# Normalising P one round later in a fused attention and soft-MoE kernel

## The chip, the cores and the metric

The kernel runs on one core of one Trainium2 chip. The time is that of one execution on the device, in microseconds (us); several executions are timed and their median is given. The kernel before takes 286.43 us (three runs, 285.88 to 286.63).

## The reference

Attention in a sliding window of 128 positions with a linear bias per head (ALiBi), for 8 batches, 8 heads, 576 positions, head size 64. Its output, 4608 tokens of 512 numbers, goes through a soft mixture of 8 experts with 4 slots each. Cut to what matters:

```python
scores = scale * q @ k.T + bias                    # masked to 0 <= i-j < 128
attn = exp(scores - max(scores))
attn = attn / (sum(attn) + 1e-9)
x = attn @ v                                       # 4608 x 512
logits = x @ phi                                   # 4608 x 32
d = softmax(logits over tokens); slot_input = d.T @ x
slot_out = relu(slot_input @ w1[e]) @ w2[e]        # for each expert
out = softmax(logits over slots) @ slot_out
```

The change touches the third line only, the division by the sum, and only when it is done.

## The kernel before, in words

The attention is a pipeline over 72 **groups**, nine for each batch: for each of the four full tiles of 128 queries two groups (two of the four blocks of 64 queries and heads at a time), and one for the tail of 64 queries. A group's scores lie in four units of 128 partitions by 128 numbers. The program is a loop of 72 **rounds**; in round i each engine works on other groups, and the order in which each engine gets its instructions is the order of the lines of the program. Every engine runs its own queue in order and waits only for the semaphores of what it reads or overwrites.

Round i, engine by engine:

- VectorE, in `softmax_front`: `merge` (L286) joins the two halves of the window of the scores of group i; `rowmax` (L300) takes the row maximum; `inverse` (L313) inverts the row sums of group i−1; `bias` (L304) makes the bias of the exponentials of group i; `normalise` (L317) multiplies P of group i−1 by the inverted sums. Behind it, when a tile of x is complete, `x_store` (L424) copies it out of its PSUM bank, and in some rounds steps of the mixture follow (L469 a maximum of logits, L496, L536, L537, L522 the accumulation of slot inputs). `filler` puts small leftover steps (L547, L548) between these.
- TensorE: `flip` (L374) transposes P of group i−3, `values` (L410) multiplies P of group i−4 by V, `scores` (L261, L270) computes the scores of group i+1; then transposes of x (L438) and logits (L456) where they are due.
- ScalarE: `split` (L380) copies the transposed P of group i−3 out of PSUM, `x_keep` (L447) and others follow, then `expo` (L359) takes the four exponentials of group i and their sums.
- GpSimd: `total` (L309) adds the epsilon to the sums of group i−1; two affine selects (L386, L388) cut the copied P of group i−3 into the part for the previous block of V and the part for its own.

Three things tie the engines together. There is one PSUM bank for x, so `values` of the next tile waits for `x_store`. There are two buffers for scores, so `scores` of group i+2 waits for `expo` of group i. And `values` waits for both selects, the first half of it for L386 and the second for L388. P itself has three buffers. A constant, `SKIP = 7`, marks the round in which TensorE's flips fall back by one round, so that from round 8 on P of group i−1 isn't flipped before round i+2.

The attention ends at about 212 us of the profiled execution; behind it the last tokens, the experts and the combination follow.

Of the kernel before, what the change touches and what calls it, by code (L numbers as in the profile page):

```python
# [10 lines left out]
F32 = mybir.dt.float32  # L11
# [13 lines left out]
P = 128  # L25
# [20 lines left out]
SKIP = 7  # L46
# [18 lines left out]
def bc(ap, dim, n):  # L65
    ap = ap.unsqueeze(dim)
    shape = list(ap.shape)
    shape[dim] = n
    return ap.to_broadcast(shape)
# [3 lines left out]
def tile_attn_softmoe(  # L73
# [16 lines left out]
    work = ctx.enter_context(tc.tile_pool(name="work", bufs=2))  # L90
# [53 lines left out]
    st = {}  # L144
    last = B - 1

    def order(b):
        return (1, 2, 3, 4, 0) if b == last else range(NT)
# [13 lines left out]
    groups = [(b, t, g) for b in range(B) for t in order(b) for g in range(2 if t < 4 else 1)]  # L162
    number = {key: i for i, key in enumerate(groups)}
    n = len(groups)
# [111 lines left out]
    ALL, LO, HI = slice(0, 4), slice(0, 2), slice(2, 4)  # L276
    EVEN, ODD = slice(0, 4, 2), slice(1, 4, 2)

    def merge(key, us=ALL):
        x = ranges(key, us).rearrange("p a (x y) -> p a x y", y=KB)  # L280
        m = x.shape[1]
        if key[1] < 4:
            to, of, keep = x[:, :, 0:6:5], x[:, :, 2:4], bc(mask.bitcast(I32), 1, m)
        else:
            to, of, keep = x[:, :, 0:8:4], x[:, :, 2:8:4], bc(bc(mask[:, 0].bitcast(I32), 1, 2), 1, m)
        nc.vector.copy_predicated(to, keep, of)  # L286

    def ranges(key, us):
        if number[key] == 0:
            return st[key]["parts"][us.start // 2].unsqueeze(1)  # L290
        return st[key]["s4"]
# [4 lines left out]
    def rowmax(key, us):  # L296
        if "nb" not in st[key]:
            st[key]["nb"] = work.tile([P, 4], F32, tag="nb", name="nb")
        st[key]["mx"] = ranges(key, us)[:, :, 4 * P - 2:4 * P]
        nc.vector.tensor_reduce(st[key]["mx"], merged(key, us), axis=AX.X, op=ALU.max, negate=True)  # L300

    def bias(key, us):
        nb = st[key]["nb"][:, us].rearrange("p (a u) -> p a u", u=2)
        nc.vector.tensor_scalar_mul(nb, st[key]["mx"], SCALE)  # L304

    def total(key, us, eng=None):
        if "rs" not in st[key]:
            st[key]["rs"] = work.tile([P, 4], F32, tag="rs", name="rs")
        (eng or nc.vector).tensor_scalar(  # L309
            st[key]["rs"][:, us], st[key]["sm"][:, us], EPS, 1.0, op0=ALU.add, op1=ALU.mult)  # L310

    def inverse(key, us):
        nc.vector.reciprocal(st[key]["rs"][:, us], st[key]["rs"][:, us])  # L313

    def normalise(key, us):
        p4, rs = st[key]["p4"][:, us], st[key]["rs"][:, us]
        nc.vector.tensor_tensor(p4, p4, bc(rs, 2, P), op=ALU.mult)  # L317

    def normalise_first(key, us):
        p4 = st[key]["p4"]  # L320
        for u in range(4)[us]:
            nc.scalar.mul(p4[:, u], p4[:, u], st[key]["rs"][:, u:u + 1])  # L322
# [3 lines left out]
    def filler():  # L326
        if fillers:
            fillers.pop(0)()

    def softmax_front(new, old):  # L330
        first, eager = number[old] == 0, 0 < number[old] < EAGER
        merge(new)
        filler()
        if not eager:
            total(old, ALL, nc.gpsimd)
        if first:
            inverse(old, ALL)
            normalise_first(old, LO)
        rowmax(new, ALL)
        filler()  # L340
        if not first and not eager:
            inverse(old, ALL)
        filler()
        bias(new, ALL)
        if eager:
            total(old, ALL)
            inverse(old, ALL)
        filler()
        normalise(old, HI if first else ALL)

    def expo(key, us=ALL):
        s = st[key]
# [421 lines left out]
    with tc.manual_schedule(engines=ORDERED):  # L774
        scores(0)
        loads(0)
        for i in range(n):
            new = groups[i]
            run("pre", i)
            if i:  # L780
                softmax_front(new, groups[i - 1])
            else:
                for us in (LO, HI):
                    merge(new, us)
                    rowmax(new, us)
                    bias(new, us)
                    expo(new, us)
            near = int(i < SKIP)
            if i + near >= FLAG and i != SKIP:
                flip(groups[i + near - FLAG])  # L790
                split(groups[i + near - FLAG])
            run("act", i)
            if i + near >= LAG and i != SKIP:
                values(groups[i + near - LAG])
                after_values(i, groups[i + near - LAG])
            if i + 1 < n:
                scores(i + 1)
            if i + 1 < n - 1:
                loads(i + 1)
            if i:  # L800
                expo(new)
            run("pe", i)
            load_weights_at(i)
            run("dve", i)
# [23 lines left out]
        split(gc)  # L828
        token_exp(end)
        total(gd, LO)  # L830
        inverse(gd, LO)
        normalise(gd, LO)
# [296 lines left out]
```

## Time and profile before

| what | value |
|---|---|
| median of three runs | 286.43 us |
| profiled execution, its own time | 286.09 us |
| its span in the profile | 284.3 us |
| TensorE busy | 257.5 us, 91% |
| VectorE busy | 218.6 us, 77% |
| ScalarE busy | 190.5 us, 67% |
| GpSimd busy | 111.7 us, 39% |
| chain of waits, by engine | TensorE 44%, VectorE 38%, ScalarE 9% |

In the profile PE is TensorE, PEld its loading of weights, DVE VectorE, ACT ScalarE, POOL GpSimd. "L317" is line 317 of the kernel before; where a row reads "A <- B: 6.6, 11, 1.0", A waited for B 6.6 us in total, 11 times, at most 1.0 us. In a row of the timeline stand the start, the duration, engine, line and operation, and in brackets how long the engine had been idle before it and who ended that. A share of the whole span says little here, since the last 70 us are other work; the rounds are read in windows of their own.

### The profile page before, as it was taken

Reading aid. Unit: us, or ns where it says so; the run is one execution under the profiler, and the core shown is the slowest. Engines: PE = TensorE matmul, PEld = TensorE weight load, DVE = VectorE, ACT = ScalarE, POOL = GpSimd, SP = SyncE. Lnnn points to the kernel's source line nnn. Section 1 sums busy time; section 2 is a strip of 40 time slices with the busy share of each in tenths; the row PEclk is TensorE's granted clock in tenths of the full one; section 3 lists DMA queues with packets and bytes.
Section 4 is the critical chain, followed back from the end, with each engine's and each line's share of the span. In section 5 each row is a group of like instructions: output and inputs, shape, how many; then the busy total and the mean of one; then the engine's idle time right before and its main releaser. Section 6 shows DMA issues by size and latency. Waiting matters only on the chain.

```text
span 284.3 us, 11675 instructions
## 1 busy us (share of the span) xinstructions
PE 257.5 (91%) x4575; PEld 180.7 (64%) x4575; DVE 218.6 (77%) x546; ACT 190.5 (67%) x780; POOL 111.7 (39%) x221
## 2 busy tenths in 40 slices
PE   7789898989899999998989998998989899999990
PEld 3567676767577677676667766766666443587750
DVE  1789998997998898899999899897973352656352
ACT  2868868887798887897897888887774411044460
POOL 3035734481574385265527526556452011000000
PEclk9999999999999999999999999999999999999996
DMA  5735368889786998889698778876565588999997
GB/s 167 238 110 153 115 173 250 255 247 295 252 277 184 303 303 262 257 265 285 221 298 283 255 236 280 268 212 218 166 213 199 172 257 296 417 416 373 376 357 295
DMA packets 36767, 72.49 MB, mean 255 GB/s; under 512 B 4413, under 2 KB 15337, under 8 KB 36713
## 3 DMA queue, kind: packets, MB, share of 16 engines
q1 hardware_dynamic: 35992, 71.25, 75.7%
q8 instruction: 36, 0.59, 0.8%
q10 hardware_dynamic: 720, 0.51, 0.6%
q14 instruction: 19, 0.15, 0.2%
HBM read 62.30 MB, written 9.44 MB: 252 GB/s over the span
## 4 chain that ended last, share of the span: by engine, by line
PE 44%; DVE 38%; ACT 9%; issue 3%; DMA 3%; POOL 1%; DVEq 0%; ACTq 0%; SPq 0%; POOLq 0%
DVE area L317 12%; DVE s L300 9%; PE xp L410 8%; ACT area L359 6%; PE op L967 5%; PE s L270 5%; DVE area L424 5%; PE hp L930 5%; DVE s L286 4%; PE po L992 4%; PE s L261 2%; PE lp L456 2%; PE pq L374 2%; DVE acc L522 2%; DMA area<-v_n 2%
## 5 line engine op out<-in xcount | busy, mean ns | idle before, releaser
L359 ACT ACTIVATE area<-s,nb 128x128 f32<-128x128 f32 x286 | 101.9, 379 | 21.6 <-DVE nb L304 20.2
L410 PE MATMUL xp<-area 128*64 128x128 f32 (+1 forms) x1104 | 71.7, 270 | 9.5 <-DVE area L424 6.6
L410 PEld LDWEIGHTS xp<-area 128*64 128x64 f32 x1104 | 54.5, 137 | 16.4 <-POOL area L388 5.0
L359 ACT ACTIVATION_READ_ACCUMULATOR area<-s,nb 128x1 f32 x286 | 62.2, 218 | 0.0
L317 DVE TENSOR_TENSOR area<-area,rs 128x512 f32<-128x512 f32 (+1 forms) x73 | 59.9, 821 | 1.7 <-ACT area L447 0.4
L270 PE MATMUL s<-kq 64*64 64x192 f32 (+2 forms) x1144 | 57.0, 316 | 0.0
L386 POOL TENSOR_SCALAR_AFFINE_SELECT area<-area 128x512 f32<-128x512 f32 (+1 forms) x57 | 42.7, 748 | 26.9 <-ACT area L380 26.3
L380 ACT COPY area<-pq 128x512 f32<-128x512 f32 (+1 forms) x72 | 42.5, 592 | 16.0 <-PE pq L374 14.3
L300 DVE TENSOR_REDUCE s<-s 128x4 f32<-128x512 f32 (+1 forms) x72 | 50.0, 694 | 2.2
L388 POOL TENSOR_SCALAR_AFFINE_SELECT area<-area 128x512 f32<-128x512 f32 (+1 forms) x57 | 46.5, 817 | 3.9
L270 PEld LDWEIGHTS s<-kq 64*64 64x64 f32 x1144 | 41.2, 139 | 3.4
L309 POOL TENSOR_SCALAR rs<-sm 128x4 f32<-128x4 f32 x70 | 13.5, 193 | 71.2 <-ACT area L359 69.8
L286 DVE COPY_PREDICATED s<-cst,s 128x256 f32<-128x256 int32 (+1 forms) x72 | 30.2, 419 | 4.8 <-PE s L270 4.4
L374 PE MATMUL pq<-unit_r,area 64*128 64x64 f32 x552 | 31.4, 234 | 1.9 <-ACT area L322 1.2
L374 PEld LDWEIGHTS pq<-unit_r,area 64*128 64x128 f32 x552 | 23.0, 140 | 11.6 <-issue 5.0
L261 PE MATMUL s<-ramp,pair_of 64*64 64x384 bf16 x286 | 27.0, 358 | 2.5 <-ACT area L359 2.0
L424 DVE COPY area<-xp 128x512 f32<-128x512 f32 (+1 forms) x38 | 24.1, 633 | 3.6 <-PE xp L410 3.4
L447 ACT COPY area<-pq 128x512 f32<-128x512 f32 x34 | 20.2, 594 | 0.3 <-PE pq L432 0.3
L261 PEld LDWEIGHTS <-pair_of 64*64 64x64 bf16 x288 | 9.5, 106 | 15.7 <-issue 12.0
L438 PEld LDWEIGHTS pq<-unit_r,area 64*128 64x128 f32 x264 | 10.7, 138 | 13.2 <-issue 11.7
L994 ACT COPY ob<-po 128x512 f32<-128x512 f32 x19 | 10.4, 592 | 11.4 <-PE po L992 11.4
L994 DVE COPY ob<-po 128x512 f32<-128x512 f32 x17 | 11.2, 686 | 6.6 <-PE po L992 4.4
(164 smaller groups left out, 276.6 us busy)
## 6 DMA issues: line engine op xcount, KB each, us to landing
w<-w SPq DMA_DIRECT2D x53, 512.0 KB, 5.4
out<-ob SPq DMA_DIRECT2D x36, 256.0 KB, 3.6
kq<-q_t SPq DMA_DIRECT2D x69, 128.0 KB, 3.3
kq<-k_t SPq DMA_DIRECT2D x32, 256.0 KB, 3.4
area<-v_n SPq DMA_DIRECT2D x31, 256.0 KB, 4.5
area<-w SPq DMA_DIRECT2D x8, 512.0 KB, 4.9
area<-v_n SPq DMA_DIRECT2D x12, 128.0 KB, 5.2
kq<-w SPq DMA_DIRECT2D x3, 512.0 KB, 5.6
```

Source lines behind the costliest of these rows:

```text
L261: nc.tensor.matmul(dst[strip], lhsT=pair_of[rows, int(t == 0), strip], rhs=src, start=True, stop=False)
L270: nc.tensor.matmul(parts[par][KB * jj:KB * jj + KB, second * u + KB * skip:second * u + WIN], lhsT=qt[rows, jj if t < 4 else j, KB * h:KB ...
L286: nc.vector.copy_predicated(to, keep, of)
L300: nc.vector.tensor_reduce(st[key]["mx"], merged(key, us), axis=AX.X, op=ALU.max, negate=True)
L317: nc.vector.tensor_tensor(p4, p4, bc(rs, 2, P), op=ALU.mult)
L359: nc.scalar.activation(s["p4"][:, u], src, AF.Exp, bias=s["nb"][:, u:u + 1], scale=SCALE, accum_out=s["sm"][:, u:u + 1],)
L374: nc.tensor.transpose(s["pt"][:, 2 * (u % 2) + u // 2, r], s["p4"][rows, u], ident[rows, rows])
L380: nc.scalar.copy(pa[:, us].rearrange("p u (r w) -> p u r w", r=2), s["pt"][:, us])
L386: nc.gpsimd.affine_select(prev, own, [[-step, m], [0, 4], [-1, KB]], ALU.is_gt, 0.0, base=-i0, channel_multiplier=1)
L388: nc.gpsimd.affine_select(own, own, [[step, m], [0, 4], [1, KB]], ALU.is_ge, 0.0, base=i0, channel_multiplier=-1)
L410: nc.tensor.matmul(xp[D * par:D * par + D, j, 0:w], lhsT=v_slot[b, t - 1 + ph][:, D * h:D * h + D], rhs=src[:, :, par, i] if t < 4 else sr ...
L424: nc.vector.tensor_copy(dst, src[:, :, 0:w])
```

## The change

The normalisation of P of group i−1 leaves its place behind the bias of round i. It is done in round i+1, behind the merge and in front of the row maximum of group i+1. This holds for rounds after round 8: round 8 has no normalisation at all, and round 71, the last, has two, the moved one behind its merge and the one of group 70 in the old place. The inverted sums live one round longer and get a third buffer. Lines of the changed kernel are four higher from L350 on (L424 is L428 there).

```diff
     def total(key, us, eng=None):
         if "rs" not in st[key]:
-            st[key]["rs"] = work.tile([P, 4], F32, tag="rs", name="rs")
+            st[key]["rs"] = work.tile([P, 4], F32, tag="rs", name="rs", bufs=3)
...
     def softmax_front(new, old):
         first, eager = number[old] == 0, 0 < number[old] < EAGER
+        late = number[new] > SKIP
         merge(new)
+        if number[new] > SKIP + 1:
+            normalise(groups[number[old] - 1], ALL)
         filler()
...
         filler()
-        normalise(old, HI if first else ALL)
+        if not late or number[new] == n - 1:
+            normalise(old, HI if first else ALL)
```

VectorE's queue in rounds 8 and 9, before. `s_0` and `s_1` are the two score buffers, `nb` the bias, `rs` the sums, `xp` the bank of x; both operands of L317 that read `area` are P.

```order
L286 COPY_PREDICATED s_0_83<-cst,s_0_83 128x4x64
L300 TENSOR_REDUCE s_0_83<-s_0_83 128x2x2
L313 RECIPROCAL rs<-rs 128x4
L304 TENSOR_SCALAR nb<-s_0_83 128x4
L317 TENSOR_TENSOR area<-area,rs 128x512
L286 COPY_PREDICATED s_1_84<-cst,s_1_84 128x2x2x64
L300 TENSOR_REDUCE s_1_84<-s_1_84 128x2x2
L313 RECIPROCAL rs<-rs 128x4
L304 TENSOR_SCALAR nb<-s_1_84 128x4
L317 TENSOR_TENSOR area<-area,rs 128x512
L424 COPY area<-xp 128x512
```

The same two rounds in the changed kernel:

```order
L286 COPY_PREDICATED s_0_83<-cst,s_0_83 128x4x64
L300 TENSOR_REDUCE s_0_83<-s_0_83 128x2x2
L313 RECIPROCAL rs<-rs 128x4
L304 TENSOR_SCALAR nb<-s_0_83 128x4
L286 COPY_PREDICATED s_1_84<-cst,s_1_84 128x2x2x64
L317 TENSOR_TENSOR area<-area,rs 128x512
L300 TENSOR_REDUCE s_1_84<-s_1_84 128x2x2
L313 RECIPROCAL rs<-rs 128x4
L304 TENSOR_SCALAR nb<-s_1_84 128x4
L428 COPY area<-xp 128x512
```

Round 8 has lost its L317; in round 9 L317 stands between merge and row maximum, and the store of x follows the bias.

VectorE's queue in round 71, the last of the loop, with the semaphores that each instruction waits for, before:

```order
L286 COPY_PREDICATED s_1_84<-cst,s_1_84 128x2x2x64 [waits PE_49]
L300 TENSOR_REDUCE s_1_84<-s_1_84 128x2x2 [waits DVE_49]
L313 RECIPROCAL rs<-rs 128x4 [waits Pool_49]
L304 TENSOR_SCALAR nb<-s_1_84 128x4 [waits DVE_49]
L317 TENSOR_TENSOR area<-area,rs 128x512 [waits DVE_49,Activation_49]
L469 TENSOR_REDUCE nm<-lg 64x1 [waits Activation_49]
```

And in the changed kernel:

```order
L286 COPY_PREDICATED s_1_84<-cst,s_1_84 128x2x2x64 [waits PE_49,Activation_49]
L317 TENSOR_TENSOR area<-area,rs 128x512 [waits DVE_49]
L300 TENSOR_REDUCE s_1_84<-s_1_84 128x2x2 [waits DVE_49]
L313 RECIPROCAL rs<-rs 128x4 [waits Pool_49]
L304 TENSOR_SCALAR nb<-s_1_84 128x4 [waits DVE_49]
L317 TENSOR_TENSOR area<-area,rs 128x512 [waits DVE_49,Activation_49]
L473 TENSOR_REDUCE nm<-lg 64x1 [waits Activation_49]
```

One L317 has come in front of the row maximum, and the old one has stayed. The merge now names ScalarE too: the exponentials of two rounds before, which read the same score buffer. The other four engines' queues are as they were.

## The prediction

> **What bounds the kernel now.** I read the windows first, then who waits for whom, then the costliest groups, then single rounds in order of time. The windows below cut out the part in which the change acts (columns: length, then busy time of PE, weight load, VectorE, ScalarE, GpSimd; the granted clock is 1.00 throughout).
>
> ```profile
> 28.00:44.00 16.00, 14.41 (x307) 10.65 (x305) 14.48 (x34) 12.54 (x55) 7.42 (x14) 1.00 0.53 157
> 44.00:70.00 26.00, 24.42 (x484) 17.97 (x484) 23.56 (x59) 21.20 (x95) 13.50 (x25) 1.00 0.84 264
> 70.00:95.00 25.00, 23.53 (x465) 17.09 (x465) 22.58 (x59) 20.57 (x90) 13.21 (x26) 1.00 0.78 248
> 95.00:120.00 25.00, 23.86 (x474) 17.32 (x470) 22.88 (x58) 20.80 (x92) 13.81 (x25) 1.00 0.84 271
> 120.00:149.00 29.00, 27.13 (x538) 19.61 (x530) 27.34 (x68) 25.09 (x110) 14.49 (x28) 1.00 0.84 271
> 149.00:175.00 26.00, 24.41 (x486) 18.15 (x486) 24.30 (x60) 21.62 (x95) 14.00 (x26) 1.00 0.84 268
> 175.00:200.00 25.00, 23.90 (x465) 17.34 (x460) 21.25 (x52) 19.11 (x83) 14.90 (x28) 1.00 0.72 223
> ```
>
> TensorE and VectorE are both over 90% busy in most of it, so the end is set by the two in turn. TensorE's idle time is the window less its busy time: 1.59, 1.58, 1.47, 1.14, 1.87, 1.59 and 1.10 us, 10.3 us together. No reordering of VectorE can win more than that. The waits say who owns it.
>
> ```profile
> PE xp L410 <- DVE area L424: 6.6, 11, 1.0
> PEld xp L410 <- POOL area L388: 5.0, 8, 1.1
> ACT area L359 <- DVE nb L304: 20.2, 31, 1.1
> DVE area L424 <- PE xp L410: 3.4, 5, 0.8
> DVE nm L469 <- ACT lg L464: 4.3, 4, 1.5
> L317 DVE TENSOR_TENSOR area<-area,rs 128x512 f32<-128x512 f32 x70 | 58.7, 838 | 1.4 <-ACT area L447 0.4
> ```
>
> The first row is the target: eleven times, 6.6 us in all, the P V product (L410) waits for the store of x (L424) to empty its bank. Before that store VectorE normalises P (L317), 838 ns on average. The second and third rows are what can be hurt: the masks on GpSimd and the exponentials, both downstream of the bias (L304).
>
> **The change part by part.** Nothing is added or removed in work: 63 normalisations (those of P of groups 7 to 69) move from behind the bias to behind the next merge, and round 8 has none. No DMA is moved, and the other engines keep their order. P is flipped two rounds after its exponentials, so the normalised P is still one round early for TensorE.
>
> *Term 1, contention.* The same instruction takes very different times. Three normalisations, and GpSimd's selects beside them:
>
> ```profile
> 132.88 0.69 DVE L317 TENSOR_TENSOR area<-area,rs 128x512 f32<-128x512 f32 x1
> ...
> 28.60 1.15 DVE L317 TENSOR_TENSOR area<-area,rs 128x512 f32<-128x512 f32 x1
> ...
> 33.97 1.12 DVE L317 TENSOR_TENSOR area<-area,rs 128x512 f32<-128x512 f32 x1
> 28.55 0.66 POOL L386 TENSOR_SCALAR_AFFINE_SELECT area<-area 128x512 f32<-128x512 f32 x1 [0.27 <-ACT area L380]
> 29.28 0.99 POOL L388 TENSOR_SCALAR_AFFINE_SELECT area<-area 128x512 f32<-128x512 f32 x1
> ...
> 33.90 0.66 POOL L388 TENSOR_SCALAR_AFFINE_SELECT area<-area 128x512 f32<-128x512 f32 x1
> ```
>
> Alone it takes 0.69 us. At 28.60 and 33.97 it stood behind a select that had begun just before it, and took 0.43 to 0.46 us more; in the first case the next select then waited in turn, 0.99 instead of 0.66. That is no accident: bias, four exponentials, copy, select add up to about a round, so selects fall where the next bias has just ended. Behind the merge, 1.0 us earlier in VectorE's round (0.33 behind the merge's start instead of 1.34, by the rows of term 2), the normalisation mostly misses them. The mean excess is 838 − 690 = 148 ns a round on VectorE, 63 × 0.148 = 9.3 us of its work; bounds 0 (contention follows it) and 9.3.
>
> The Trainium skill, "SBUF — State Buffer", section "Who interferes with whom", has it that a VectorE instruction with two SBUF inputs and a GpSimd instruction that reads SBUF exclude each other for the whole of the one that was first. The rows at 33.90 and 33.97 agree: 33.90 + 0.66 = 34.56, and the late one ended 0.53 behind that. By that rule a meeting in the new place costs as much as one in the old.
>
> *Term 2, a gap that is filled.* The row maximum reads what the merge wrote. A filler that doesn't read it, already there in one round of eight, shows what an instruction costs in between:
>
> ```profile
> 123.83 0.42 DVE L286 COPY_PREDICATED s<-cst,s 128x256 f32<-128x256 int32 x1
> 124.29 0.70 DVE L300 TENSOR_REDUCE s<-s 128x4 f32<-128x512 f32 x1
> 124.89 0.17 DVE L313 RECIPROCAL rs<-rs 128x4 f32<-128x4 f32 x1
> 125.02 0.16 DVE L304 TENSOR_SCALAR nb<-s 128x4 f32<-128x4 f32 x1
> 125.17 0.76 DVE L317 TENSOR_TENSOR area<-area,rs 128x512 f32<-128x512 f32 x1
> 125.85 0.42 DVE L286 COPY_PREDICATED s<-cst,s 128x256 f32<-128x256 int32 x1
> 126.18 0.28 DVE L547 TENSOR_REDUCE cs<-ln 128x4 f32<-128x132 f32 x1
> 126.38 0.68 DVE L300 TENSOR_REDUCE s<-s 128x4 f32<-128x512 f32 x1
> ```
>
> Merge to maximum is 0.46 us bare, but 0.33 to the independent filler. So a normalisation of 0.60 from start to start (0.69 less the overlap of 0.09 that most neighbours show) costs about 0.33 + 0.60 − 0.46 = 0.47 in the new place, 0.60 in the old: 0.13 a round. Bounds 0 and 0.13.
>
> [...]
>
> *The price.* Each bias, and so each set of exponentials, comes 0.47 us later behind its merge. Where VectorE is the late one this changes nothing, because the work has only gone round the loop: the bias then follows the previous store directly. Where the merge itself waited for scores, or where the store waited for TensorE (3.4 us, five times) or the maximum of the logits for ScalarE (4.3 us, four times), the normalisation was cover for that wait; now it stands behind it, and 0.47 is paid on the path bias, exponentials, copy, selects, P V.
>
> *One stretch followed through.* Rounds 8 to 11, row by row:
>
> ```profile
> 28.41 0.13 DVE L304 TENSOR_SCALAR nb<-s 128x4 f32<-128x4 f32 x1
> 28.42 0.51 PE L270 MATMUL s<-kq 64*64 64x64 f32 x16
> 29.67 0.42 DVE L286 COPY_PREDICATED s<-cst,s 128x256 f32<-128x256 int32 x1
> 32.04 0.68 DVE L424 COPY area<-xp 128x512 f32<-128x512 f32 x1
> 32.87 1.09 PE L410 MATMUL xp<-area 128*64 128x128 f32 x16 [0.87 <-DVE area L424]
> 37.43 0.68 DVE L424 COPY area<-xp 128x512 f32<-128x512 f32 x1
> 38.26 1.15 PE L410 MATMUL xp<-area 128*64 128x64 f32 x32 [0.37 <-DVE area L424]
> ```
>
> Round 8 loses its normalisation, so the merge of 29.67 starts once the scores end (28.93) at about 29.0. Its normalisation, at 29.3, still meets the select of 29.28 and ends near 30.5; maximum, reciprocal and bias end at 31.4, and the store starts there instead of at 32.04: P V at 32.2 instead of 32.87. Two rounds on the next store can start at 36.4 instead of 37.43; by then P V waits only for its own queue, and 38.26 becomes 37.25. Gain 1.0 us of the 1.59 that TensorE had idle.
>
> I followed 120 to 175 us the same way. These waits are there for the taking:
>
> ```profile
> 129.51 1.09 PE L410 MATMUL xp<-area 128*64 128x128 f32 x16 [0.97 <-DVE area L424]
> 149.17 1.21 PE L410 MATMUL xp<-area 128*64 128x128 f32 x16 [0.61 <-DVE area L424]
> 154.68 1.09 PE L410 MATMUL xp<-area 128*64 128x128 f32 x16 [0.37 <-DVE area L424]
> 174.60 1.22 PE L410 MATMUL xp<-area 128*64 128x128 f32 x16 [0.57 <-DVE area L424]
> 136.39 1.15 DVE L317 TENSOR_TENSOR area<-area,rs 128x512 f32<-128x512 f32 x1
> ```
>
> At 129.51 almost nothing comes of it, because the later bias makes the selects late as well. By 149.17 the store is 0.5 earlier, by 174.60 another 0.85. As shares of idle time that is 0.5/1.87 and 0.85/1.59, about 0.4 on average; the four windows that I did not follow have fewer such waits, so I take 0.35 of all six: 0.35 × 8.75 = 3.1 us.
>
> *The end.* The last bias goes straight into the last exponentials, and TensorE waits behind them:
>
> ```profile
> 210.03 0.37 ACT L359 ACTIVATE area<-s,nb 128x128 f32<-128x128 f32 x1 [0.61 <-DVE nb L304]
> 212.06 0.66 PE L369 MATMUL pq<-unit_r,area 128*128 128x128 f32 x4 [1.14 <-ACT area L447]
> ```
>
> There the later bias is paid: 0.47, less a little contention, 0.4 us lost.
>
> Sum: −1.0 − 3.1 + 0.4 = −3.7 us. The profiled execution took 286.09 us, 1.79 around its span of 284.3; 286.09 − 3.7 = 282.4. The median shown, 286.43, is 0.34 above it, so on that footing **282.7 us**.
>
> **The rivals.** *No difference.* Five waits of the store for P V and four of the logits' maximum for ScalarE lose their cover: 9 × 0.47 = 4.2 us would eat the whole gain, and TensorE, 90% busy, has little to give: 286.2. For it: the nine waits. Against: they are followed by rounds in which VectorE catches up, as at 136.39, where 0.46 of contention goes. *Contention follows.* The selects shift with the bias and meet the normalisation behind the merge, as they do at 29.3 above. Then term 1 vanishes and only round 8, term 2 and the early stores remain, about −1.2: 285.2. *Slower, the masks take over.* Its place is the P V of the rounds in which TensorE runs without a break; eight waits for L388 (5.0 us) and six for L386 (3.7) are in the trace now.
>
> ```profile
> PEld xp L410 <- POOL area L386: 3.7, 6, 0.9
> ```
>
> If the later bias reaches the selects undiminished, 14 × 0.47 = 6.6 us; the selects give 0.33 back where they no longer wait, so 14 × 0.14 = 2.0 at least, and nothing won at the store: 288.4 to 293, say 289. It decides once the selects' slack before P V is under 0.47 in most rounds. Against: the second select is only needed for the second half of P V, 0.6 us later. *The change does something else*: excluded by the order, where the store follows the bias.
>
> **How the numbers follow.** Forecast 0.57, contention follows 0.13, no difference 0.14, slower 0.16. The forecast's own range is 280.1 to 284.5 (0.65 or 0.15 of the idle time in place of 0.35). With the rivals it is 280.1 to 287.2. This kernel's measurement tells about 0.3% from no change, so faster means under 285.57 and slower over 287.29. In the order of the cases, faster: 0.55 + 0.08 + 0.01 + 0 = 0.64. Same: 0.02 + 0.04 + 0.11 + 0.01 = 0.18. Slower: 0 + 0.01 + 0.02 + 0.15 = 0.18.
>
> **What would show it.** Right: L317's mean near 0.72 (now 838 ns), L386 and L388 near 0.70; waits of L410 for L424 under 3 us; merge to maximum about 0.93; TensorE's busy time per window unchanged while its idle time falls. Wrong: L317 still above 0.80 (contention followed), L410's waits for L388 and L386 above 10 us (the masks took over), or ScalarE's wait for L304 up by more than 10 us with TensorE's idle time unchanged (cover lost).

## The result

The changed kernel takes 284.20 us (median of 22 runs, 282.56 to 285.93), the kernel before 285.69 us beside it (22 runs, 284.06 to 286.96). The ratio is 0.9949, with a 95% interval of 0.9930 to 0.9968: 1.5 us faster, between 0.9 and 2.0. The prediction said 3.7 us. The direction is right, the size is under half. In what follows, a ratio r is turned into microseconds as (r − 1) × 285.7; behind it in brackets stands its 95% interval. Medians are over all executions of a kernel, ratios leave out the few slow ones.

The profiled execution of the changed kernel took 285.77 us, 1.57 above its own median, with a span of 284.0 us; from 28 to 212 us its clock is 1.00 as before. Its rounds can be read even so: from the merge (L286) of round 8 to that of round 71 it takes 1.46 us less than the profiled execution before (180.15 against 181.61), and what it lost lies behind the last merge (77.0 us to the end of the span, against 75.7). Lines of the changed kernel are four higher from L350 on: the store is L428, P V L414, the selects L390 and L392, the scaling of the logits L553.

### The profile page after: what moved, and what is told of

Same layout as the page of the kernel before. It is cut to its first block, busy times and chain, and to the rows that moved or that the text cites. A ratio compares the mean times of both kernels' runs of the same rounds, so it can differ in the third digit from the quotient of the medians.

```text
span 284.0 us, 11653 instructions
## 1 busy us (share of the span) xinstructions
PE 256.5 (90%) x4575; PEld 179.0 (63%) x4575; DVE 202.0 (71%) x546; ACT 190.8 (67%) x780; POOL 106.4 (37%) x221
## 4 chain that ended last, share of the span: by engine, by line
PE 67%; DVE 11%; ACT 7%; POOL 4%; DMA 4%; issue 3%; DVEq 0%; ACTq 0%
PE xp L414 17%; PE s L270 11%; PE op L971 5%; PE s L261 5%; PE pq L378 5%; PE hp L934 5%; ACT area L363 5%; PE po L996 4%; PE pq L442 3%; DVE s L300 3%; DVE area L317 3%; PE lp L460 2%; POOL area L392 2%; PE ap L518 2%; DVE s L286 2%
## 5 line engine op out<-in xcount | busy, mean ns | idle before, releaser
L414 PE MATMUL xp<-area 128*64 128x128 f32 (+1 forms) x1104 | 72.4, 271 | 6.7 <-POOL area L392 2.8
L414 PEld LDWEIGHTS xp<-area 128*64 128x64 f32 x1104 | 54.4, 137 | 14.0 <-POOL area L392 4.6
L363 ACT ACTIVATION_READ_ACCUMULATOR area<-s,nb 128x1 f32 x286 | 61.0, 213 | 0.0
L270 PE MATMUL s<-kq 64*64 64x192 f32 (+2 forms) x1144 | 55.6, 311 | 0.3 <-DMA kq<-k_t 0.3
L317 DVE TENSOR_TENSOR area<-area,rs 128x512 f32<-128x512 f32 (+1 forms) x73 | 51.6, 707 | 0.3
L309 POOL TENSOR_SCALAR rs<-sm 128x4 f32<-128x4 f32 x70 | 17.9, 255 | 79.2 <-ACT area L363 72.7
L390 POOL TENSOR_SCALAR_AFFINE_SELECT area<-area 128x512 f32<-128x512 f32 (+1 forms) x57 | 38.4, 673 | 21.6 <-ACT area L384 20.5
L286 DVE COPY_PREDICATED s<-cst,s 128x256 f32<-128x256 int32 (+1 forms) x72 | 30.5, 424 | 17.2 <-PE s L270 16.6
L392 POOL TENSOR_SCALAR_AFFINE_SELECT area<-area 128x512 f32<-128x512 f32 (+1 forms) x57 | 41.2, 723 | 3.9
L270 PEld LDWEIGHTS s<-kq 64*64 64x64 f32 x1144 | 39.6, 136 | 4.1 <-DMA kq<-k_t 0.7
L428 DVE COPY area<-xp 128x512 f32<-128x512 f32 (+1 forms) x38 | 24.1, 635 | 6.6 <-PE xp L414 6.6
L261 PE MATMUL s<-ramp,pair_of 64*64 64x384 bf16 x286 | 26.1, 351 | 2.9 <-ACT area L363 2.6
```

Of the source, the lines that this page charges most:

```text
L261: nc.tensor.matmul(dst[strip], lhsT=pair_of[rows, int(t == 0), strip], rhs=src, start=True, stop=False)
L270: nc.tensor.matmul(parts[par][KB * jj:KB * jj + KB, second * u + KB * skip:second * u + WIN], lhsT=qt[rows, jj if t < 4 else j, KB * h:KB ...
L363: nc.scalar.activation(s["p4"][:, u], src, AF.Exp, bias=s["nb"][:, u:u + 1], scale=SCALE, accum_out=s["sm"][:, u:u + 1],)
L390: nc.gpsimd.affine_select(prev, own, [[-step, m], [0, 4], [-1, KB]], ALU.is_gt, 0.0, base=-i0, channel_multiplier=1)
L392: nc.gpsimd.affine_select(own, own, [[step, m], [0, 4], [1, KB]], ALU.is_ge, 0.0, base=i0, channel_multiplier=-1)
L414: nc.tensor.matmul(xp[D * par:D * par + D, j, 0:w], lhsT=v_slot[b, t - 1 + ph][:, D * h:D * h + D], rhs=src[:, :, par, i] if t < 4 else sr ...
```

## The profile after

The waits of the changed kernel over its whole span (who waited for whom: us in total, times, longest):

```profile
DVE s L286 <- PE s L270: 16.6, 24, 1.8
ACT area L363 <- DVE nb L304: 21.6, 32, 1.2
DVE area L428 <- PE xp L414: 6.6, 11, 0.9
POOL ln L553 <- DVE rs L313: 3.2, 6, 0.9
PE xp L414 <- POOL area L392: 2.8, 6, 0.6
PE xp L414 <- POOL area L390: 1.2, 4, 0.5
PE xp L414 <- DVE area L428: 0.4, 1, 0.4
```

The last row answers the target of the prediction: P V waits 0.4 us for the store, where it waited 6.6. In its place stand the two rows above: 4.0 us for the selects, where TensorE's own wait for them was 0.3. (The rows of the prediction with 5.0 and 3.7 us are those of the weight load, PEld; that wait is 8.8 us now.) And the first row says that VectorE has changed sides: the merge waits 24 times for scores, 16.6 us, where it waited 8 times, 4.4 us. VectorE is now early and TensorE late. The row of L553 will matter; the same wait was 1.3 us in three places before. With the places that the profile puts down to the line next to it, L552 (L548 before), it is 3.4 us in seven places against 1.6 in five.

The normalisation and the two selects at their full size (count, busy time, mean in ns, idle before):

```profile
L317 DVE TENSOR_TENSOR area<-area,rs 128x512 f32<-128x512 f32 x70 | 50.4, 720 | 0.1
L390 POOL TENSOR_SCALAR_AFFINE_SELECT area<-area 128x512 f32<-128x512 f32 x55 | 37.5, 683 | 19.4 <-ACT area L384 18.4 <-PE xp L414 0.3
L392 POOL TENSOR_SCALAR_AFFINE_SELECT area<-area 128x512 f32<-128x512 f32 x55 | 40.2, 730 | 3.8
```

Most of the contention is gone, as term 1 had it: the normalisation fell from 838 to 720 ns, close to the 0.69 us of an undisturbed one, the selects from 761 and 828 to 683 and 730. VectorE's busy time fell from 218.6 to 202.0 us. But the windows, cut as in the prediction, show that TensorE made little of it:

```profile
28.00:44.00 16.00, 15.48 (x331) 11.64 (x329) 13.20 (x36) 13.80 (x60) 6.64 (x15) 1.00 0.58 176
44.00:70.00 26.00, 24.24 (x482) 17.73 (x478) 21.21 (x60) 20.76 (x92) 13.02 (x26) 1.00 0.83 261
70.00:95.00 25.00, 24.13 (x471) 16.89 (x463) 20.94 (x59) 20.48 (x92) 12.90 (x25) 1.00 0.78 255
95.00:120.00 25.00, 23.96 (x476) 17.41 (x474) 21.16 (x58) 21.11 (x94) 12.08 (x25) 1.00 0.83 265
120.00:149.00 29.00, 26.93 (x528) 19.63 (x529) 24.51 (x68) 24.88 (x107) 14.87 (x31) 1.00 0.88 274
149.00:175.00 26.00, 24.84 (x500) 18.24 (x500) 21.34 (x59) 22.05 (x95) 13.51 (x27) 1.00 0.86 272
175.00:200.00 25.00, 23.78 (x465) 17.39 (x461) 18.80 (x52) 19.18 (x84) 13.43 (x26) 1.00 0.69 209
```

In the first window TensorE's idle time falls from 1.59 to 0.52 us. In the six others it falls from 8.75 to 8.12 us only (1.76, 0.87, 1.04, 2.07, 1.16, 1.22), where the prediction had 35% of it, 3.1 us, going. So the early stretch works and the middle does not.

What stands in the way in the middle is seen in one place, 125 to 129 us of the changed kernel, across four engines in order of time:

```profile
125.38 0.60 ACT L384 COPY area<-pq 128x512 f32<-128x512 f32 x1
126.14 0.17 DVE L552 RECIPROCAL cs<-cs 128x4 f32<-128x4 f32 x1
126.39 0.40 POOL L553 TENSOR_TENSOR ln<-ln,cs 128x128 f32<-128x128 f32 x1 [0.61 <-DVE rs L313]
126.74 0.66 POOL L390 TENSOR_SCALAR_AFFINE_SELECT area<-area 128x512 f32<-128x512 f32 x1
127.35 0.68 DVE L317 TENSOR_TENSOR area<-area,rs 128x512 f32<-128x512 f32 x1
127.47 1.08 POOL L392 TENSOR_SCALAR_AFFINE_SELECT area<-area 128x512 f32<-128x512 f32 x1
128.61 0.66 PE L414 MATMUL xp<-area 128*64 128x128 f32 x8 [0.49 <-POOL area L392]
```

The copy that the first select needs is done at 125.98. The select begins at 126.74, because GpSimd stands at L553, the scaling of the logits over slots: it waits 0.61 us for a reciprocal of VectorE, and both selects are queued behind it. The profile names L313, but by the program L553 reads only what L552 writes, and in all seven places of the attention it starts 0.08 to 0.09 us behind the end of L552. Late by 0.7 us, the second select then starts 0.12 behind a normalisation and takes 1.08 instead of 0.66, and P V waits. The chain of waits of the changed kernel through this place (start, length, what):

```profile
124.40 0.43 DVE s L286
124.83 0.59 DVE area L317
125.43 0.20 DVE cs L551
125.63 0.61 DVE s L300
126.23 0.08 DVE cs L552
126.31 0.07 DVE rs L313
126.39 0.40 POOL ln L553
```

From there it goes on through the two selects to P V, as in the rows above. The moved normalisation, 0.59 us, is a link of this chain: it stands ahead of the reciprocal that L553 waits for. There are seven L553 in the attention, at 55.16, 81.12, 101.53, 126.39, 146.51, 171.51 and 192.76 us. P V waits for a select ten times, at 56.23 and 57.30, 82.18 and 83.25, 102.60 and 103.67, 128.61, 147.58 and 148.65, and 173.84: each of the ten stands behind one of the first six. In the kernel before L549 waited too, but at this place P V was held by the store anyway:

```profile
127.22 0.40 POOL L549 TENSOR_TENSOR ln<-ln,cs 128x128 f32<-128x128 f32 x1 [0.16 <-DVE cs L548]
```

There the wait was 0.16 us, and the P V of that round began at 129.51 with 0.97 us of waiting for L424 (the prediction quotes the row).

## The experiments

I came to this reading late. At first I took the masks to be late because the bias is: bias, exponentials, copy, select. The first eleven runs were made with that theory; they are told first.

**Which part, and which stretch.** The store directly behind the bias, with the P that was normalised before, one round no later:

```diff
-        normalise(old, HI if first else ALL)
+        if number[new] <= SKIP:
+            normalise(old, HI if first else ALL)
...
                 after_values(i, groups[i + near - LAG])
+            if i > SKIP:
+                normalise(groups[i - 1], ALL)
```

> From round 8 on the store of x stands directly behind the bias, and the normalisation of the same P (group i-1) directly behind the store: the store is early and the bias is not late. Theory A (the later bias made the masks late and ate the gain in the middle): the waits of P V for the masks stay at or below those of the kernel before (5.0 and 3.7 us), the waits for the store fall under 1.5 us, and the time falls by 2.5 to 3.5 us. Theory B (TensorE has nothing to give in the middle, whoever is early): about the same as the change, 1.2 to 1.8 us less. Theory C (what the change won was contention with GpSimd, not the early store): the normalisation stays above 0.80 us on average here, and the gain is under 0.7 us.

Measured: 284.21 us, ratio 0.9953 (0.9929 to 0.9977), as much as the whole change. The waits of P V for the store are gone here too, and the contention stays:

```profile
L317 DVE TENSOR_TENSOR area<-area,rs 128x512 f32<-128x512 f32 x70 | 60.0, 857 | 0.1
PE xp L411 <- POOL area L389: 2.7, 8, 0.4
```

So an early store without term 1 wins 1.3 us, and the change with both wins 1.5. That is the time of theory B; the times of A and C are missed.

The change in rounds 8 to 16 alone:

```diff
-        late = number[new] > SKIP
+        late = SKIP < number[new] < 16
         merge(new)
-        if number[new] > SKIP + 1:
+        if SKIP + 1 < number[new] <= 16:
             normalise(groups[number[old] - 1], ALL)
...
-        if not late or number[new] == n - 1:
+        if not late:
```

> The change in rounds 8 to 16 alone (round 16 carries two normalisations), the old order from there on. Theory A and B both put the gain in the stretch from 28 to 48 us and a loss of about 0.5 us at the last bias: 1.5 to 2.2 us less than before, at least as good as the whole change. Theory C (contention falls evenly over 63 rounds): 9/63 of the gain, 0.2 to 0.4 us less.

Measured: 283.44 us, 0.9924 (0.9899 to 0.9950), −2.2 us. And from round 16 on alone:

```diff
-        late = number[new] > SKIP
+        late = number[new] > 15
         merge(new)
-        if number[new] > SKIP + 1:
+        if number[new] > 16:
             normalise(groups[number[old] - 1], ALL)
```

> The change from round 16 on alone, the old order before. Theory A and B: nothing in the middle and the loss at the last bias, so 0 to 0.6 us more than before. Theory C: 1.0 to 1.4 us less.

Measured: 286.0 us, 1.0026 (1.0001 to 1.0051), +0.7 us (0.0 to 1.5). The two parts add up to the change, −2.2 + 0.7 = −1.5. The early stretch wins more than was predicted. In the trace of the change round 17 begins at 51 us, ahead of the first L553 at 55. All the rest together wins nothing, and likely loses a little.

One round later, but in the old place behind the bias:

```diff
         merge(new)
-        if number[new] > SKIP + 1:
-            normalise(groups[number[old] - 1], ALL)
...
         filler()
+        if number[new] > SKIP + 1:
+            normalise(groups[number[old] - 1], ALL)
         if not late or number[new] == n - 1:
```

> Normalised one round later as in the change, but in the old place behind the bias, in front of the store: the delay without the move. All theories: within 0.5 us of before, less the one normalisation that round 8 no longer has (at most 0.6 us less). If it gains as much as the change, it is the delay that counts and not the place.

Measured: 281.56 us, 0.9868 (0.9841 to 0.9895), −3.8 us. I had meant this as a control that does nothing. The delay alone, without an earlier store, wins more than the change. Its group of normalisations, and one meeting with a select:

```profile
L317 DVE TENSOR_TENSOR area<-area,rs 128x512 f32<-128x512 f32 x70 | 53.3, 763 | 0.0
132.58 0.13 DVE L304 TENSOR_SCALAR nb<-s 128x4 f32<-128x4 f32 x1
132.62 0.68 DVE L317 TENSOR_TENSOR area<-area,rs 128x512 f32<-128x512 f32 x1
132.72 1.11 POOL L390 TENSOR_SCALAR_AFFINE_SELECT area<-area 128x512 f32<-128x512 f32 x1 [0.27 <-ACT area L384]
```

The normalisation of an older P doesn't read the reciprocal of 0.2 us before. It starts 0.08 us behind the bias (median), where it was 0.15, and so comes in ahead of the select (by 0.10 here) where it lost by 0.05 and 0.07 in the rows of the prediction. From round 9 on 14 are over 0.75 us, where there were 31. The loser in such a meeting is now GpSimd: the selects are no faster than before in all (804 and 797 ns, against 761 and 828), but P V waits only 0.9 us for one.

**Without the selects.** If the masks hold the change back, it must win more with no masks. These three kernels leave out both selects, so the window isn't cut and both halves of P V read the same P:

```diff
-        if t:
-            own, prev = (
...
-        s.update(pd=pa, pp=pp)
+        s.update(pd=pa, pp=pa)
```

Of the kernel before, of the change, and of the delay alone:

> The kernel before without the two selects on GpSimd (the copied P goes to both parts, so the window is not cut): no contention for the normalisation and no masks for P V to wait for. The base of the two that follow; all theories: 3 to 8 us under before.

> The changed kernel without the two selects. Theory A (the late bias hurts through the masks): without masks it is 1.5 to 3 us under the kernel before without selects. Theory C (what the change won was contention): at best equal to the kernel before without selects, or slower by 0.5 to 2 us, because only the late bias is left. Theory B (TensorE has nothing to give): equal within 0.7 us.

> One round later behind the bias, without the two selects. Theory D, if it is the port that counts: within 1 us of the kernel before without selects. If the 0.07 us that the normalisation no longer waits for the reciprocal count by themselves (63 rounds, 4.4 us of VectorE): 2 to 4 us under it.

Measured: 279.55 us (0.9768, 0.9743 to 0.9793), 276.70 us (0.9683, 0.9657 to 0.9708) and 277.72 us (0.9709, 0.9685 to 0.9733). Without selects the change wins 2.4 us by the ratios (2.9 by the medians) although it has no contention to win back then, and the front place is no worse than the one behind the bias (better by 0.7 us by the ratios, whose intervals overlap; 1.0 by the medians); with selects it is worse by 2.3. So what is in the way comes through the selects. The scaling of the logits still waits in the changed kernel without selects:

```profile
POOL ln L544 <- DVE rs L313: 3.1, 6, 0.9
```

That is as long as in the change, but no select is queued behind it there. The delay alone wins 1.7 here, less than the 2 that one theory asked for and more than the 1 of the other: part of its 3.8 has nothing to do with the selects.

**Store ahead of the older P.** Bias, store, then the P of two rounds before:

```diff
-        if number[new] > SKIP + 1:
-            normalise(groups[number[old] - 1], ALL)
...
-        if not late or number[new] == n - 1:
+        if number[new] <= SKIP:
             normalise(old, HI if first else ALL)
...
                 after_values(i, groups[i + near - LAG])
+            if i > SKIP + 1:
+                normalise(groups[i - 2], ALL)
+            if i == n - 1:
+                normalise(groups[i - 1], ALL)
```

> Both at once: one round later (P of group i-2) and behind the store, so bias, store, normalisation. Theory D (the delay wins because the normalisation no longer waits for the reciprocal just ahead of it, starts 0.08 us behind the bias and gets the shared memory port before the next select): behind the store that start is lost in every second round, so L317 goes back over 0.78 us on average and the time is 1.5 to 3 us under before, no better than the delay alone (3.6 us under). Theory A (the early store is what counts): at least as good as the delay alone, 3.5 to 4.5 us under before.

Measured: 296.38 us, 1.0359 (1.0329 to 1.0389), 10 us slower. Both theories expected a gain. The trace shows a wait that neither had:

```profile
PE pq L375 <- DVE area L317: 17.7, 24, 1.2
```

The normalisation now waits behind the store, which waits for P V, and the next flip waits for the normalisation. That is a loop of VectorE and TensorE waiting for each other. The normalisation takes 802 ns, less than the 838 before, so contention is not the reason.

**The end, and the early stretch alone in front.** The change, with the last rounds behind the bias:

```diff
-        if number[new] > SKIP + 1:
+        if number[new] > SKIP + 1 and number[new] < n - 4:
             normalise(groups[number[old] - 1], ALL)
...
+        if number[new] > SKIP + 1 and not number[new] < n - 4:
+            normalise(groups[number[old] - 1], ALL)
```

> The change, but in the last four rounds the normalisation (still of P of group i-2) stands behind the bias, so that the last bias is not late. If the end costs what the prediction said (0.4 us): 1.7 to 2.1 us under before, where the change is 1.5 under. If the end costs nothing: 1.5 under.

The front place up to round 16, behind the bias from 17 on (the same edit with `number[new] < 17`):

> One round later everywhere; in front of the row maximum up to round 16, behind the bias from 17 on. Theory A (in the early stretch the front place gains, later it loses through the late bias): 3.6 to 4.3 us under before, at least as good as behind the bias everywhere (3.6). If the front place costs everywhere: 2.5 to 3.4.

Measured: 282.88 us (0.9903, 0.9872 to 0.9934), and 281.08 us (0.9836, 0.9805 to 0.9867). The first wins 1.3 us on the change, give or take 1.0; the second wins 3.2. Both win more than was expected (2.8 and 4.7 us under before). Both agree with front being good early and bad later, and neither says why.

**Is it the reciprocal?** The delay alone, with the reciprocal taken along directly ahead of the normalisation, so that the one waits for the other again:

```diff
-        if not first and not eager:
+        if not first and not eager and (not late or number[new] == n - 1):
             inverse(old, ALL)
...
         filler()
+        if number[new] > SKIP + 1:
+            inverse(groups[number[old] - 1], ALL)
+            normalise(groups[number[old] - 1], ALL)
```

> The delay of one round behind the bias (3.6 us under before), but the reciprocal of the same P is taken along and stands directly ahead of the normalisation, behind the bias. The normalisation waits for it again and starts no earlier against the select than in the kernel before, while the bias comes one reciprocal (0.13 us) earlier and waits for no sum. Theory D (the 0.07 us earlier start behind the bias and the port are the gain): L317 back to 0.80 us or more and less than 1.5 us under before. If instead it is the early bias or the wait for the sums that counts: 3 us or more under before.

Measured: 284.61 us, 0.9959 (0.9940 to 0.9978). Of the 3.8 us of the delay 1.2 are left. The normalisation starts 0.28 us behind the bias (median), L317 takes 791 ns on average against 763, and the flips wait 4.0 us for it, against 2.0. So most of the delay's gain goes when the normalisation stands behind its reciprocal again. The 791 ns are just under the 0.80 us that the theory of contention asked for, and the reciprocal has moved too, so how much the meetings with selects make of this stays open.

**GpSimd's queue.** Now the theory read from the chain above: L553 waits for VectorE, and the selects wait behind L553. First, the change with the normalisation behind the bias in those rounds alone in which steps of L551 to L553 are waiting, those of the seven scalings:

```diff
+        free = not fillers
         merge(new)
-        if number[new] > SKIP + 1:
+        if number[new] > SKIP + 1 and free:
             normalise(groups[number[old] - 1], ALL)
...
+        if number[new] > SKIP + 1 and not free:
+            normalise(groups[number[old] - 1], ALL)
```

> The change, but in the seven or so rounds that carry the steps L551, L552 and L553 (the scaling of the logits over slots) the normalisation stands behind the bias again. Theory A (the later bias reaches the selects through exponentials and copy, in all rounds alike): seven rounds of 63 are a ninth of the effect, 283.9 to 284.3 us, and P V's waits for the selects (2.8 and 1.2 us) stay within 0.8 us of that. Theory B (GpSimd's queue: L553 waits for VectorE's reciprocals, which the normalisation in front delays by 0.47 us, and both selects of the round stand behind L553): those waits fall under 1.2 us together and the time to 281 to 283 us.

Measured: 282.58 us, 0.9883 (0.9863 to 0.9903), −3.3 us, and P V's waits for the selects are down to 1.0 us; theory B had both. These few rounds double the gain, by 1.9 us, give or take 0.8. Second, VectorE's order left as in the change, and L553 put behind the two selects of its round on GpSimd:

```diff
+    held = []
...
         s.update(pd=pa, pp=pp)
+        while held:
+            held.pop(0)()
...
-            lambda: mul(slots(k), slots(k), bc(cs[:, 0:m], 2, NS), op=ALU.mult),
+            lambda: (held.append if k < end else lambda f: f())(
+                lambda: mul(slots(k), slots(k), bc(cs[:, 0:m], 2, NS), op=ALU.mult)),
```

> The change, but GpSimd's L553 is issued behind the two selects of its round instead of ahead of them; VectorE's order is that of the change. Theory A: 284 us, as the change, P V's waits for the selects 3 to 4 us in all. Theory B: those waits under 1.2 us together, the long second selects of those rounds (1.0 to 1.1 us) gone in part, the time 280.5 to 282.5 us.

The same on the kernel before, and on the one with the front place up to round 16:

> The kernel before with the same move of L553 (L549 there) behind the selects. Both theories: little, since P V hardly waits for selects there; 0 to 0.8 us faster, 284.9 to 285.7 us. If it gains as much as the same move gains on the change (over 1.5 us), the move has a worth of its own and says nothing on what the change lost.

> The normalisation one round later everywhere, in front of the row maximum up to round 16 and behind the bias from 17 on, and L553 behind the selects. Theory A: as without the move of L553, 281.1 us. Theory B: from round 17 on nothing delays L552 in that kernel, so little again, 280.3 to 281.1 us; if the front place is harmless once L553 is out of the way, the change with L553 moved comes within 1 us of this one.

These three leave out the eighth scaling, which falls after the last round. Measured: 279.69 us (0.9798, 0.9773 to 0.9823), 286.97 us (1.0040, 1.0017 to 1.0063) and 280.43 us (0.9807, 0.9779 to 0.9835). The first wins more than either theory expected, the second is outside what both expected. The same move of seven small instructions wins 4.3 us on the change and loses 1.1 on the kernel before. On the kernel that has the normalisation behind the bias in those rounds it wins 0.8, with intervals that overlap. So what it gives the change is what the change had lost there. The first of the three is also no worse than the third: with L553 out of the way the front place is harmless in the middle.

Where the move costs the kernel before its 1.1 us is seen in its trace:

```profile
PE xp L413 <- DVE area L427: 8.1, 11, 1.0
148.14 0.66 POOL L387 TENSOR_SCALAR_AFFINE_SELECT area<-area 128x512 f32<-128x512 f32 x1 [0.27 <-ACT area L381]
148.19 1.15 DVE L317 TENSOR_TENSOR area<-area,rs 128x512 f32<-128x512 f32 x1
```

P V waits 8.1 us for the store in all, instead of 6.6. In the kernel before, the scaling held the first select back, and in this round the normalisation began first (147.70, 0.73 us, the select at 147.83). Without the scaling in front the select begins first, the normalisation takes 1.15 us, and the store behind it is late: P V waits 1.04 us for it, where it waited 0.61.

With all eight scalings (the last one issued when the rounds are over), and then with the last four rounds behind the bias as well:

```diff
     def drain():
         while fillers:
             filler()
+        while held:
+            held.pop(0)()
```

> As the run with L553 behind the selects (which left out the eighth scaling of the logits, after the last round), now with all eight. Theory B: the eighth stands in the tail, so the last merge stays near 200.7 us and the time near 279.7, 279.3 to 280.5 us. If the eighth scaling had carried the gain, the last merge would be unchanged and the time 281 to 284 us.

> The same, and the last four rounds normalise behind the bias. If the later bias costs the end the 0.4 us predicted, 279.3 us against 279.7; if the larger gain of the earlier run with the last four rounds behind the bias (1.3 us) was the end's own, 278.4 us.

Measured: 279.34 us, 0.9777 (0.9735 to 0.9819), −6.4 us; and 278.41 us, 0.9735 (0.9696 to 0.9773), −7.6 us, the best kernel of this study. Of the first, the place that corresponds to the one shown above, and the four middle windows:

```profile
123.76 0.66 POOL L391 TENSOR_SCALAR_AFFINE_SELECT area<-area 128x512 f32<-128x512 f32 x1 [0.27 <-ACT area L385]
124.49 0.66 POOL L393 TENSOR_SCALAR_AFFINE_SELECT area<-area 128x512 f32<-128x512 f32 x1
125.12 0.88 POOL L557 TENSOR_TENSOR ln<-ln,cs 128x128 f32<-128x128 f32 x1
...
70.00:95.00 25.00, 24.64 (x484) 17.44 (x484) 21.75 (x59) 20.84 (x91) 11.98 (x26) 1.00 0.84 265
95.00:120.00 25.00, 24.43 (x488) 17.85 (x488) 22.02 (x59) 21.51 (x96) 12.62 (x26) 1.00 0.84 272
120.00:149.00 29.00, 28.46 (x568) 21.17 (x566) 26.03 (x71) 25.65 (x110) 15.82 (x33) 1.00 0.87 277
149.00:175.00 26.00, 25.49 (x517) 18.84 (x515) 22.65 (x60) 22.36 (x99) 12.55 (x26) 1.00 0.84 271
```

Both selects take 0.66 us directly behind the copy, the scaling follows them when nobody waits, and no product of P V waits for a select any more. TensorE's idle time in these four windows is 0.36, 0.57, 0.54 and 0.51 us, 1.98 together, where it was 6.07 before and 5.14 with the change.

The price can also be read round by round. Take the start of the merge (L286) of each round and subtract it from that of the same round in the kernel before; this is how far ahead a kernel is. Below is how much that lead grows or shrinks from one round to the next, at the seven scalings (one profiled execution of each kernel, us):

| rounds | 19–20 | 28–29 | 35–36 | 44–45 | 51–52 | 60–61 | 67–68 |
|---|---|---|---|---|---|---|---|
| the change | −0.88 | −0.88 | −0.83 | −0.77 | −0.88 | −0.88 | −0.61 |
| L553 behind the selects, all eight | −0.12 | −0.10 | +0.09 | +0.21 | −0.01 | −0.09 | +0.33 |

The first six, those behind which P V waits, cost the change 5.1 us together, and nothing (−0.02) with L553 out of the way. From round 8 to round 71 the leads grow by 1.5 and 7.2 us.

At the end, the wait of TensorE for the last exponentials in these two kernels, first the one with the front place to the end:

```profile
205.14 0.66 PE L374 MATMUL pq<-unit_r,area 128*128 128x128 f32 x4 [1.50 <-ACT area L454]
```

```profile
203.59 0.66 PE L376 MATMUL pq<-unit_r,area 128*128 128x128 f32 x4 [1.06 <-ACT area L456]
```

The profile names the copy (x_keep) that ScalarE has queued behind those exponentials. The wait is 0.44 us shorter, close to the predicted 0.4; the medians differ by 0.9 us, with ranges that overlap (278.98 to 281.12, 277.24 to 279.7).

## Why the prediction was right, and where it was wrong

- **What bounds the kernel:** right. P V's waits for the store, and VectorE's work ahead of it, were the bound, and the store did move to behind the bias.
- **Term 1, contention:** right in size. L317 came to 720 ns ("near 0.72"), the selects to 683 and 730 ("near 0.70"). But that work was not what the end hung on: the kernel with L553 behind the selects is 4.9 us faster than the change with L317 at 762 ns, and the store-first kernel wins nearly as much as the change at 857.
- **Term 2, the filled gap:** right. Merge to maximum was predicted at 0.93 us; rows of the changed kernel:

```profile
127.01 0.43 DVE L286 COPY_PREDICATED s<-cst,s 128x256 f32<-128x256 int32 x1
127.35 0.68 DVE L317 TENSOR_TENSOR area<-area,rs 128x512 f32<-128x512 f32 x1
127.95 0.69 DVE L300 TENSOR_REDUCE s<-s 128x4 f32<-128x512 f32 x1
```

  It is 0.94. Had the normalisation started as late as an instruction that reads the merge's result, it would be 0.46 + 0.60 = 1.06. The Trainium skill, "VectorE: DVE Perf Modes", section "The DRAIN you can't avoid", says that a next instruction that is not held starts earlier than when the pipe is empty. The trace agrees: the normalisation, which doesn't read the result, starts 0.34 behind the merge's start, the row maximum in the kernel before, which does, 0.46.
- **The stretch followed through:** right row by row, a little small in sum. Merge predicted at about 29.0, store at 31.4, P V at 32.2:

```profile
29.00 0.43 DVE L286 COPY_PREDICATED s<-cst,s 128x256 f32<-128x256 int32 x1 [0.53 <-PE s L270]
31.12 0.68 DVE L428 COPY area<-xp 128x512 f32<-128x512 f32 x1
31.95 1.09 PE L414 MATMUL xp<-area 128*64 128x128 f32 x16 [0.36 <-DVE area L428]
```

  The next P V came at 36.91 (predicted 37.25), and TensorE's idle time up to 44 us fell by 1.07 us (predicted 1.0). The early rounds alone gave 2.2 us (1.4 to 2.9): in the trace of the change the lead grows by 1.2 us to the merge of round 12 and by 2.2 to that of round 16, at 47 us, where the stretch had stopped at 44.
- **The middle, "0.35 × 8.75 = 3.1 us":** here the prediction failed. The step that was wrong is the price ahead of it: the later VectorE work was followed along "bias, exponentials, copy, selects, P V", and "the other engines keep their order" was taken to mean that GpSimd is not concerned. What the normalisation delays on VectorE is not the bias alone but the reciprocal L552 too. GpSimd's L553 waits for it, and the selects wait behind L553. That wait was in the profile before, as

```profile
POOL ln L549 <- DVE rs L313: 1.3, 3, 0.7
```

  and is not in the prediction; it stood at 1.3 us, and at the place shown above P V was waiting for the store anyway. Behind the normalisation it grew to 3.2 us (3.4 with the place put down to L552), with ten waits of P V after it. Its price is 0.9949 − 0.9777 = 1.7%, 4.9 us, give or take 1.3. That is the price of L553 ahead of the selects in the change, its own 0.40 us and its wait together; putting the normalisation back behind the bias in those rounds gives back 1.9, and gives up the front place there. With L553 out of the way the change is worth 6.4 us, so the 3.1 us of the middle was too little by itself: 3.7 lay between two larger numbers of opposite sign.
- **The end, 0.4 us lost:** TensorE's wait went from 1.14 us (quoted in the prediction) to 1.50 with the change, and was 0.44 shorter with the last rounds behind the bias; the times differ by 0.9 and, in the other pair, by 1.3, give or take 1.0, so they can't tell 0.4 from more.
- **The rivals:** "the masks take over" named the right victim and the wrong road. P V's waits for the selects did replace those for the store (0.3 to 4.0 us), though in six rounds, not "in most". That its price, 2.0 to 6.6 us, contains the 4.9 is luck, since it was counted from other waits; its "nothing won at the store" was wrong, and so its sign. "Contention follows" is excluded by 720 ns. "No difference" lies outside the interval, 0.9 to 2.0 us faster; of the waits that it counted, the store's for P V did grow, from 3.4 to 6.6 us, but on VectorE, which now has time.
- **The range:** 284.20 us lies inside the forecast's 280.1 to 284.5 by luck. That range was counted from 286.43, and the kernel before ran at 285.69 beside the changed one. As a change it says 1.9 to 6.3 us less, and 1.5 is outside.
- **The signs:** all signs of "right" came true but the last. That one could not come true as it was written: the idle time was worked out as the window less the busy time, so it can't fall in a fixed window with the busy time unchanged. What it meant, less idle time, showed in the first window and hardly in the others (8.75 to 8.12 us). None of the signs of "wrong" fired: the selects' waits, by the weight load as there, were 8.8 us, under 10. Only the idle time is measured where the time is made.

What stays open: how the delay's 3.8 us divide between the contention and the gap behind the reciprocal is shown only roughly, by 1.7 us without selects and 1.2 us left when the reciprocal goes along. That its own scalings wait less (2.0 us by both lines, against 3.4 in the change) helps to explain why it beats the change, and not why it beats the kernel before.

## What to carry to other kernels

When an instruction is moved ahead of others in a queue, list every instruction that now comes later, and for each the waits of other engines on it, the small and rare ones too; then look at what is queued behind those waits. A wait that costs little today, with critical work queued behind it, can be the place where a reordering is paid, as it was here. And a mean duration that falls is not a gain: look whether the engine that sets the end has less idle time.

## What the runs showed of the hardware

- A lead of under a tenth of a microsecond is enough to decide who pays when VectorE's normalisation and GpSimd's select meet. Select first by 0.07 us: 0.66 and 1.12 us. Normalisation first by 0.10 us: 0.68 and 1.11 us. The sum is nearly the same, and what matters is which of the two has time to lose. The scaling of the logits on GpSimd is no exception: beside a normalisation begun at 125.06 it took 0.88 us, alone 0.40. The Trainium skill, "SBUF — State Buffer", section "Who interferes with whom", has it that such a pair exclude each other, the later one waiting out the first. These rows agree on who loses, not quite on how much: the later ones lost 0.43 and 0.45 us, where the first had 0.59 and 0.58 still to run.
- An instruction that doesn't need the one just before it starts 0.04 to 0.08 us behind a small one; one that needs the reciprocal directly ahead of it starts 0.20 behind that. Normalising one round later, with the same instructions in the same place, took 3.8 us off the kernel.
